# A convolution with a gated layer on one Trainium2 core: residual of two tile pairs moved to VectorE, gate weights loaded before four input tiles, idle products in halves, and a new order

## The chip, the cores and the metric

The kernel runs on one core of one Trainium2 chip. The core has five engines with instruction streams of their own: TensorE (PE, with its weight loads listed as PEld), VectorE (DVE), ScalarE (ACT), GpSimd (POOL) and SyncE (SP), which here only issues transfers. The metric is the device time of one execution in microseconds. A timing is the median of several executions; a profile is one execution more, recorded by the hardware profiler.

## The reference

The input `A_u` has 2048 rows of 512 channels. It is normalised by rows, and three things are added: the input itself, a long convolution over the rows (one kernel per channel, made of 128 complex modes), and a gated layer of inner width 1792.

```python
x  = A_u                                   # 2048 x 512
xn = _layernorm(x)
# convolution: kernel per channel from A, B, C and dt
logdA = exp(log_dt)[:, None] * (A_re + 1j * A_im)
P  = exp(logdA[:, :, None] * arange(L))
K  = einsum("dn,dnl,dn->dl", Cc, P, dt * Bc).real
y  = irfft(rfft(pad(xn)) * rfft(pad(K)))[:L] + xn * Dskip
# gated layer
h  = sigmoid(xn @ w_gate) * (xn @ w_up)    # 2048 x 1792
out = x + y + h @ w_down
```

All inputs are bfloat16, and so is the output.

## The kernel before

**Planner and order.** The kernel does not issue instructions as its functions run. Each step is recorded by `pl.add(engine, cost, fn, deps, prio, acq, rel)` as an operation with a number (966 of them), with the operations it depends on and the buffer slots that it takes and gives back. `run()` then walks a list of all numbers, `ORDER`, which is written out in the file; slots are handed out first in, first out along the list. The list is thus the program order of every engine and queue at once; semaphores are set from the dependences. The costs and due times that the operations carry are not used once the list is there. Pools that matter here: `gu`, four PSUM banks for the products of the gated layer; `s`, two PSUM pairs (1024 columns) for all else; `ot`, three output tiles.

**Which engine.** Three tuples move single steps between engines. `UEV` lists those of the 56 up products (4 row groups of 512 rows by 14 tiles of the inner width) that ACT copies from PSUM to SBUF (L1072) before DVE multiplies them with the gate (L1076); for the others DVE reads the PSUM bank in the multiplication. `ON_DVE` lists the operations among copies (L285 on DVE, L287 on ACT), casts (L660, L662) and row normalisations that run on DVE rather than on ACT. `FIN_ACT` lists those of six tile pairs of the output for which the other summand is brought in by PE.

**Stages.** All loads of the start (L430 to L470) go to SP's queue, one behind the other. While they run, `keep_warm` (L516) gives PE idle products of 128×512 into a bank that nobody reads. `layernorm` (L531) normalises the rows: tiles x0 to x3 (128 rows each) early, and transposes them by PE into `xnT`; x4 to x15 go out to a scratch in DRAM and come back transposed. The parameters (`par`, two loads) pass through a chain on DVE and ACT (L609 to L634, `f_w0` and `f_g` among it) to the first power of the modes, and a ladder of squarings (L664 to L679) makes eleven more; casts put them into the tables `W`. The convolution is a transform in two steps: first products over row tiles (`fx`, L685 on) are stored to `z_scr`; the convolution kernel's terms are built by DVE in four parts (c = 0 to 3, L747 to L843); then for each of two channel halves (p = 0, 1) and eight units a tile of `z_scr` is loaded and transformed (L882), swapped, multiplied with the kernel's transform (L904, L909, L913), transformed back (`fv`, L926), copied from PSUM (L287) and stored to `v_scr`. From `v_scr` the tiles are loaded again (`reload`, L963 to L974) for the last step (`s2_mm`, L985 and L988). Between all these, PE works on the gated layer: gate products (L1036), up products (L1060), down products (L1105), group by group of 512 rows.

**The end.** For the first three row groups the down products are copied to `glu_sb`, the input rows are added to them by a transfer that accumulates, and `final` (L990) joins them, pair by pair of tiles, with the last step of the convolution:

```python
res = glu_sb[:, 2 * t:2 * t + 2, :] if t < 4 else ...
on = t in FIN_ACT
def fi():
    for r in range(2):
        T.matmul(bank(sl, r), ident[:], res[:, r, :], start=True, ...)
...
if on:      # ACT copies the sum out of PSUM (L1007)
else:       # DVE adds res to the PSUM sum (L1011)
```

With a pair in `FIN_ACT`, two products with an identity matrix (L999) put `res` into PSUM first, the convolution's products add to it, and ACT copies the pair out. Otherwise DVE adds `res` while it reads the pair. The last row group's down products go into the same bank as their convolution sums, and DVE adds the input rows (L1125); its last tile is done in two halves of 256 columns. Output stores go out on SP's queue, the very last on ACT's.

Of the kernel before, what the change touches and what calls it, by code (L numbers as in the profile page):

```python
# [44 lines left out]
FIN_ACT = (1, 3, 5,)  # L45
# [133 lines left out]
def _consts():  # L179
# [19 lines left out]
UEV = (0, 6, 7, 9, 11, 12, 13, 14, 15, 16, 17, 18, 19, 21, 23, 24, 25, 26, 28, 29, 30, 31, 32, 33, 34, 35, 36, 37, 38, 39, 40, 41, 43, 44, 46, 47, 49, 52, 54, 55,)  # L199
ON_DVE = (88, 91, 106, 108, 123, 124, 125, 139, 140, 186, 196, 197, 200, 201, 203,)  # L200
ON_ACT = (2,)
ORDER = [
# [43 lines left out]

class _Op:
    __slots__ = ("alt", "tab", "eng", "cost", "fn", "prio", "acq", "rel", "dma", "left", "users", "ready", "start", "done", "seq", "mode")

class _Slot:  # L250
    __slots__ = ("pool", "idx")

    def __init__(self, pool, idx=None):
        self.pool = pool
        self.idx = idx
# [62 lines left out]
def kernel(  # L318
# [197 lines left out]
    def keep_warm(n, prio):  # L516
        wsl = _Slot("gu")
# [229 lines left out]
    for c in range(4):  # L747
# [11 lines left out]
        n = 1  # L759
# [435 lines left out]
```

## Time and profile before

| | us |
|---|---|
| median of three timed runs | 217.75 |
| the three runs | 217.75, 217.63, 219.24 |
| the profiled execution | 219.51 |
| its span, first to last instruction | 217.6 |

The difference of 1.9 us between the profiled execution and its span lies around the instructions. The granted PE clock is full (1.00) in the whole span. An engine's busy time is the union of its instructions; a wait is time in which the engine stood with its next instruction blocked, put down to what released it. In lists of instructions the form is: engine, line, operation, result tile, operand tiles, shape and count; in the timeline, start and length stand in front. "SPq" and "ACTq" are issues of transfers; a transfer's landing is told from its issue.

### The profile page before, as it was taken

The page shows a single profiled execution, that of the slowest core. Times are in us where ns is not written, and L with a number is a line of the kernel's source. Part 1 is how long each engine was busy: PE and PEld are TensorE (multiplying, and loading weights), DVE is VectorE, ACT ScalarE, POOL GpSimd, SP SyncE. Part 2 cuts the span into 40 slices and gives each one's busy share as a digit, 9 for nine tenths or more (in the row PEclk, how much of TensorE's full clock was granted, in tenths as well). Part 3 has the DMA queues.
Part 4 walks back from the last instruction along what each step waited for, and adds up shares of the span by engine and source line. Part 5 has one row for each costly group of instructions (what it writes and reads, how often), then busy time and mean ns, then how long its engine had stood idle before and what let it go on. Part 6 is the DMA issues. An engine that isn't in the chain of part 4 may idle for free.

```text
span 217.6 us, 4946 instructions
## 1 busy us (share of the span) xinstructions
PE 209.0 (96%) x1876; PEld 104.0 (48%) x1876; DVE 193.8 (89%) x438; ACT 179.5 (83%) x286; POOL 18.8 (9%) x40
## 2 busy tenths in 40 slices
PE   7979999999999999989999999999999999999894
PEld 2435444444444454435455565445546556544463
DVE  3989999999999999999999999999999999970433
ACT  3799999999999999869989999976897999960111
POOL 1410202002100020012000002010800000000000
PEclk9999999999999999999999999999999999999999
DMA  6999936001463689865697679929959969984974
GB/s 186 316 369 390 299 116 146 0 3 48 145 156 97 233 249 156 264 143 105 166 271 202 183 224 209 239 79 216 216 116 252 282 188 263 267 245 139 269 256 166
DMA packets 51530, 42.80 MB, mean 197 GB/s; under 512 B 16434, under 2 KB 43571, under 8 KB 51507
## 3 DMA queue, kind: packets, MB, share of 16 engines
q1 hardware_dynamic: 50338, 40.60, 63.8%
q0 software_dynamic: 864, 1.57, 5.5%
q10 hardware_dynamic: 304, 0.33, 0.6%
q8 instruction: 14, 0.23, 0.4%
q14 instruction: 10, 0.07, 0.1%
HBM read 25.97 MB, written 12.85 MB: 178 GB/s over the span
## 4 chain that ended last, share of the span: by engine, by line
PE 64%; DMA 17%; ACT 8%; SPq 7%; issue 2%; DVE 0%; ACTq 0%
PE bank L1060 18%; PE bank L1036 16%; PE bank L1105 10%; PE pair L904 7%; SPq L421 7%; DMA wu_sb<-in_B_w_up_dram 5%; PE pair L926 4%; ACT big L287 4%; DMA z_scr<-big 3%; DMA big<-big 3%; DMA big<-z_scr 2%; DMA v_scr<-big 2%; PE pair L882 2%; PE pair L820 2%; ACT us_sb L1072 2%
## 5 line engine op out<-in xcount | busy, mean ns | idle before, releaser
L287 ACT ACTIVATE big<-pair 128x1024 bf16<-128x1024 f32 x64 | 66.2, 1060 | 4.9 <-PE pair L926 1.5
L1060 PE MATMUL bank<-xnT,wu_sb 128*128 128x512 bf16 x224 | 54.5, 380 | 0.5 <-DMA wu_sb<-in_B_w_up_dram 0.4
L1036 PE MATMUL bank<-xnT,wg_sb 128*128 128x512 bf16 (+1 forms) x220 | 50.7, 368 | 1.9 <-DMA wg_sb<-in_B_w_gate_dram 1.8
L1105 PE MATMUL bank<-wd_sb,hT_sb 128*128 128x512 bf16 (+1 forms) x238 | 50.4, 367 | 0.0
L1036 PEld LDWEIGHTS <-wg_sb 128*128 128x128 bf16 x236 | 22.2, 98 | 26.9 <-issue 2.5
L1105 PEld LDWEIGHTS <-hT_sb 128*128 128x128 bf16 x238 | 22.6, 98 | 25.2 <-issue 1.9
L1060 PEld LDWEIGHTS <-wu_sb 128*128 128x128 bf16 x224 | 20.6, 98 | 25.2 <-issue 3.0
L1048 ACT ACTIVATE hT_sb<-bank 128x512 bf16<-128x512 f32 x52 | 30.9, 636 | 1.2 <-PE bank L1036 1.1
L735 DVE TENSOR_TENSOR big<-big 128x1024 bf16<-128x1024 bf16 (+4 forms) x40 | 26.8, 670 | 0.3 <-ACT big L287 0.2
L736 DVE TENSOR_TENSOR big<-big 128x1024 bf16<-128x1024 bf16 (+4 forms) x40 | 26.7, 667 | 0.0
L1072 ACT ACTIVATE us_sb<-bank 128x512 bf16<-128x512 f32 x40 | 25.9, 648 | 0.3
L909 DVE TENSOR_TENSOR big<-big 128x2048 bf16<-128x2048 bf16 x16 | 19.5, 1218 | 0.6 <-PE pair L926 0.3
L904 PE MATMUL pair<-big 128*128 128x256 bf16 x160 | 19.8, 273 | 0.0
L789 ACT ACTIVATE sq_sb<-big 128x256 bf16<-128x256 bf16 (+2 forms) x20 | 13.8, 691 | 5.1 <-DVE big L741 4.9
L904 PEld LDWEIGHTS <-big 128*128 128x128 bf16 x160 | 15.4, 98 | 4.9 <-issue 1.0
L1076 DVE TENSOR_TENSOR hT_sb<-hT_sb,us_sb 128x512 bf16<-128x512 bf16 x40 | 16.5, 418 | 0.4 <-ACT us_sb L1072 0.3
L740 DVE TENSOR_TENSOR big<-big 128x512 bf16<-128x512 bf16 (+4 forms) x40 | 16.5, 414 | 0.1
L741 DVE TENSOR_TENSOR big<-big 128x512 bf16<-128x512 bf16 (+4 forms) x40 | 16.5, 413 | 0.0
L1007 ACT ACTIVATE big<-pair 128x1024 bf16<-128x1024 f32 x3 | 3.1, 1023 | 15.2 <-PE pair L985 12.4
L895 DVE COPY big<-big 32x1024 bf16<-32x1024 bf16 x32 | 13.4, 419 | 0.6
L1011 DVE TENSOR_TENSOR big<-pair,glu_sb 128x1024 bf16<-128x1024 f32 x2 | 2.5, 1226 | 11.7 <-PE pair L985 8.1
L541 DVE BATCH_NORM_STATS2 stats<-big 128x6 f32<-128x512 bf16 x15 | 9.8, 682 | 3.4 <-DMA big<-in_A_u_dram 3.4
(104 smaller groups left out, 244.3 us busy)
## 6 DMA issues: line engine op xcount, KB each, us to landing
big<-c_E SPq DMA_DIRECT2D x16, 320.0 KB, 3.9
z_scr<-big SPq DMA_DIRECT2D x16, 256.0 KB, 2.9
big<-z_scr SPq DMA_DIRECT2D x16, 256.0 KB, 4.9
v_scr<-big SPq DMA_DIRECT2D x16, 256.0 KB, 3.1
big<-in_A_u_dram SPq DMA_DIRECT2D x4, 512.0 KB, 8.2
big<-big SPq DMA_DIRECT2D x32, 64.0 KB, 3.6
wu_sb<-in_B_w_up_dram SPq DMA_DIRECT2D x2, 896.0 KB, 10.7
wd_sb<-in_B_w_down_dram SPq DMA_DIRECT2D x1, 1792.0 KB, 15.1
```

The source lines that it names most:

```text
L287: nc.scalar.activation(out=get(out), in_=get(in_), func=ACT.Identity)
L735: V.tensor_tensor(out=wide(outp), in0=wide(lo), in1=mre, op=ALU.mult)
L736: V.tensor_tensor(out=wide(tb()), in0=wide(lo), in1=mim, op=ALU.mult)
L740: V.tensor_tensor(out=outp[:, :, 0], in0=outp[:, :, 0], in1=tb()[:, :, 1], op=opr)
L741: V.tensor_tensor(out=outp[:, :, 1], in0=outp[:, :, 1], in1=tb()[:, :, 0], op=opi)
L904: T.matmul(two(sk)[:, o:o + DW], es()[:, g, kt, :], kTv[p][:, :, kt, :], start=kt in (0, NKT - 1), stop=kt >= NKT - 2)
L909: V.tensor_tensor(out=pp().rearrange("p q h m -> p (q h) m"), in0=xx().rearrange("p q h m -> p (q h) m"), in1=kb()[:, 0:2 * DW].unsqueeze( ...
L1036: T.matmul(bank(sl, k % 2)[:, c0:c1], w[:, kt, k * 128:(k + 1) * 128], xnT[:, grp, kt, c0:c1], start=(kt == 0), stop=(kt == KT - 1))
L1048: S.activation(out=hT_sb[:, hs.idx, k % 2, :], in_=bank(sl), func=ACT.Sigmoid)
L1060: T.matmul(bank(sl), wu_sb[:, kt, k * 128:(k + 1) * 128], xnT[:, grp, kt, :], start=(kt == 0), stop=(kt == KT - 1))
L1072: S.activation(out=us_sb[:, us.idx, :], in_=bank(sl), func=ACT.Identity)
L1105: T.matmul(bank(po)[:, 0:c[1] - c[0]], hT_sb[:, hts[k // 2].idx, k % 2, jj * 128:(jj + 1) * 128], wd_sb[:, k, c[0]:c[1]], start=first and ...
```

## The change

Six things differ:

1. `FIN_ACT` goes from (1, 3, 5) to (5,): tile pairs 1 and 3 lose their identity products (two operations, four matmuls), and DVE adds `res` for them in place of ACT's copy.
2. `UEV` has 38 members rather than 40, and others.
3. `ON_DVE` is another set: the ladder's cast of k = 10, one copy of `gc` and a seed copy go to ACT; three seed copies come to DVE; of the row normalisations, tiles 4 and 6 are on DVE in place of 5 and 7, and tile 8 in place of 12.
4. `keep_warm` does its products in halves of 256 columns where it has more than one.
5. The order of the loads on SP's queue. Before: x0, x1, x2–3, `dskr`, `par` (A), identity, x4–7 (512 KB), first gate piece (896 KB, the largest), `par` (B and C), the two other gate pieces, up weights first half, second half, x8–11, x12–15, down weights. After: x1, x0, x2–3, `par` (A), identity, first gate piece, x4–7, `par` (B and C), the other gate pieces, up weights second half, x8–11, the table S1, x12–15, up weights first half, down weights; `dskr` comes later.
6. The rest of the list is reordered on every engine. On PE the idle product at 27.81 us moves to the start, with six instead of four between the transposes. On SP, near the end, the stores of the last three units to `v_scr` stand directly behind one another, ahead of the loads that bring `v_scr` back for the second channel half; before, a load of 384 KB stood ahead of the last store.

```diff
-FIN_ACT = (1, 3, 5,)
+FIN_ACT = (5,)
...
-UEV = (0, 6, 7, 9, 11, 12, 13, 14, 15, 16, 17, 18, 19, 21, 23, 24, 25, 26, 28, 29, 30, 31, 32, 33, 34, 35, 36, 37, 38, 39, 40, 41, 43, 44, 46, 47, 49, 52, 54, 55,)
-ON_DVE = (88, 91, 106, 108, 123, 124, 125, 139, 140, 186, 196, 197, 200, 201, 203,)
+UEV = (1, 7, 9, 10, 11, 12, 13, 15, 16, 17, 18, 19, 20, 22, 24, 25, 28, 29, 30, 31, 32, 33, 34, 35, 36, 37, 38, 39, 40, 41, 42, 46, 48, 49, 50, 52, 53, 55,)
+ON_DVE = (88, 105, 107, 122, 123, 124, 125, 140, 197, 198, 199, 200, 201, 202, 203,)
 ORDER = [
-    0, 1, 2, 14, 28, 38, 26, 29, 27, 3, 30, 39, 49, 32, 31, 40, 33, 41, 35, 18, 34, 4, 42, 43, 50, 24, 10, 44, 19,
...
-    956, 864, 962, 872, 869, 868, 963, 870, 957, 871, 960, 873, 874, 875, 961, 964, 965]
+    1, 28, 18, 0, 24, 2, 3, 26, 29, 38, 27, 30, 31, 32, 39, 33, 4, 49, 40, 34, 41, 43, 35, 22, 42, 50, 36, 44, 51,
...
+    863, 954, 870, 867, 868, 866, 871, 955, 869, 960, 961, 959, 872, 962, 873, 963]
...
         def fn():
-            for _ in range(n):
-                T.matmul(bank(wsl), glu_sb[:, 0, 0:128], glu_sb[:, 0, :], start=True, stop=True)
+            w = 256 if n > 1 else 512
+            for c in range(0, 512 * n, w):
+                cs = slice(c % 512, c % 512 + w)
+                T.matmul(bank(wsl)[:, cs], glu_sb[:, 0, 0:128], glu_sb[:, 0, cs], start=True, stop=True)
```

The operations behind the second dropped one keep their place in the kernel's text and have numbers lower by one or two, so the two lists cannot be compared number by number at their end. Lines behind L519 have numbers higher by two in the changed kernel.

82 rows, old and new, of the table ORDER are left out of this document.

## The prediction

> **What bounds the kernel now.** I read the page first, then the waits of TensorE (PE), then the three stages as windows, then the chain in order of time at both ends.
>
> ```profile
> span 217.6 us, 4946 instructions
> PE 209.0 (96%) x1876; PEld 104.0 (48%) x1876; DVE 193.8 (89%) x438; ACT 179.5 (83%) x286; POOL 18.8 (9%) x40
> ...
> GB/s 186 316 369 390 299 116 146 0 3 48 145 156 97 233 249 156 264 143 105 166 271 202 183 224 209 239 79 216 216 116 252 282 188 263 267 245 139 269 256 166
> ...
> PE 64%; DMA 17%; ACT 8%; SPq 7%; issue 2%; DVE 0%; ACTq 0%
> ```
>
> PE is busy for 96% and carries most of the chain; what is left of the chain is mostly transfers. Where PE waits:
>
> ```profile
> PE bank L1036 <- DMA wg_sb<-in_B_w_gate_dram: 1.8, 1, 1.8
> ...
> PE pair L985 <- DMA big<-v_scr: 0.8, 1, 0.8
> ```
>
> ```profile
> 10.00:190.00 180.00, 176.82 (x1653) 87.34 (x1654) 176.91 (x401) 167.66 (x271) 16.24 (x29) 1.00 0.70 191
> ...
> 200.00:214.50 14.50, 13.61 (x121) 8.46 (x119) 5.80 (x7) 3.07 (x3) 0.00 (x0) 1.00 0.77 231
> ```
>
> The columns are the stretch, its length, then busy time of PE, weight load, DVE, ACT and POOL, and the granted clock. From 10 to 190 us DVE is as full as PE: each is idle about 3.1 us of 180 (180 − 176.9), ACT 12.3. From 200 us on, only PE is full (13.61 of 14.5); DVE has 8.7 and ACT 11.4 idle. So work taken from PE shortens the tail at once, while in the middle PE and DVE have to gain together.
>
> **The start: gate weights ahead of input rows.**
>
> ```profile
> 2.11 0.34 SPq L421 DMA_DIRECT2D dskr<-in_A_Dskip_dram  x1
> ...
> 3.84 0.43 SPq L421 DMA_DIRECT2D wg_sb<-in_B_w_gate_dram  x1
> ...
> 4.87 2.69 SPq L421 DMA_DIRECT2D wg_sb<-in_B_w_gate_dram  x2
> ```
>
> ```profile
> DMA to landing us min/median/max: 8.6/10.4/10.9
> ```
>
> ```profile
> 1.43 6.87 PE L521 MATMUL bank<-glu_sb 128*128 128x512 bf16 x18 [1.43 <-POOL rz L515]
> ...
> 12.50 3.63 PE L1036 MATMUL bank<-xnT,wg_sb 128*128 128x512 bf16 x16 [1.80 <-DMA wg_sb<-in_B_w_gate_dram]
> ...
> 18.13 2.77 PE L1036 MATMUL bank<-xnT,wg_sb 128*128 128x256 bf16 x20
> 21.32 1.04 PE L1060 MATMUL bank<-xnT,wu_sb 128*128 128x512 bf16 x4 [0.42 <-DMA wu_sb<-in_B_w_up_dram]
> ...
> 27.81 0.38 PE L521 MATMUL bank<-glu_sb 128*128 128x512 bf16 x1
> 28.03 1.89 PE L1060 MATMUL bank<-xnT,wu_sb 128*128 128x512 bf16 x8
> ```
>
> The first gate weights are issued at 3.84 and land 8.6 later, at 12.45; PE starts on them at 12.50 after waiting 1.80. The change puts x4–7 (512 KB) behind them. At the 369 to 390 GB/s of those slices 512 KB take 1.4 us, so they land at about 11.1; the removed issue of dskr (0.34) goes too, but the data, not the issues, are late here. The transposed rows allow it:
>
> ```profile
> 10.35 0.68 DVE L573 COPY xnT<-pair 128x1024 bf16<-128x1024 bf16 x1
> 10.95 1.87 DVE L541 BATCH_NORM_STATS2 stats<-big 128x6 f32<-128x512 bf16 x3
> ...
> 13.79 1.29 DVE L609 TENSOR_TENSOR big<-big 128x512 f32<-128x512 bf16 x2 [0.90 <-DMA big<-in_A_par_dram]
> ...
> 15.61 0.68 DVE L634 TENSOR_TENSOR big<-big 128x512 f32<-128x512 f32 x1
> ...
> 18.14 0.69 DVE L541 BATCH_NORM_STATS2 stats<-big 128x6 f32<-128x512 bf16 x1
> ```
>
> xnT is complete at 11.03 (10.35 + 0.68). So the first gate starts near 11.2, 1.3 earlier. Not all is kept: the other two gate pieces have as many bytes ahead of them as before and land at about 15.3 and 16.5 (4.87 + 10.4; the second issue + 10.9), so four gates of 0.86 (3.63 for four) are through at 14.7 and PE waits some 0.6 and then 0.3. The up weights come in two halves of 896 KB, 2.4 us each at that rate. Before, the half that PE asks for first came second, and PE waited for it at 21.32 (0.42). Now it comes first and lands about 16.5 + 2.4 = 18.9, ahead of the first up product, which the gates hold until about 19.4: no wait. The other half goes behind x8–15 (1 MB): 18.9 + 2 × 1.4 + 2.4 ≈ 24.1, and the new order asks for it some two microseconds later; if that is too late, PE waits there instead. Moreover the idle product at 27.81 leaves the busy stretch: 0.22, by the start of the next row (28.03 − 27.81). Sum at 30 us: 1.3 − 0.9 + 0.42 + 0.22 ≈ 1.0 of lead. Bounds: 0 if the queue serves the pieces side by side, 2.4 if both waits (1.80 + 0.42) and the product go.
>
> What it costs: x4–7 now land where the weights landed, near 12.45. DVE took three of their statistics from 10.95 while it waited for the parameters anyway (0.90 until 13.79). With all four (0.6 each) behind 12.45, the parameter products (f_g, L609) start near 14.9 instead of 13.79, and the ladder's start, over at 16.29 (15.61 + 0.68), ends near 17.4: 1.1 later, of which 0.6 is the fourth statistic (at 18.14 before) done ahead and so given back. The rest, 0.5, is lost time of a full engine. PE's next need of the ladder is the kernel generation, with gate and up products between as cover.
>
> Halving the idle products keeps their columns, and all of them now sit in the first 11 us, where PE waits for rows; so do the two more idle products between the transposes and x1 loaded ahead of x0 (three equal loads in one row of issues). Priced at zero; the cover is that wait for the first gate weights. If it were gone, the two products would cost 0.22 each. That they no longer warm the array I count in no case: the granted clock is 1.00 in the windows, with gaps of 1.80 us before.
>
> **The middle.** Work changes hands both ways.
>
> ```profile
> L1072 ACT ACTIVATE us_sb<-bank 128x512 bf16<-128x512 f32 x40 | 25.9, 648 | 0.3
> L1076 DVE TENSOR_TENSOR hT_sb<-hT_sb,us_sb 128x512 bf16<-128x512 bf16 x40 | 16.5, 418 | 0.4 <-ACT us_sb L1072 0.3
> ...
> L1076 DVE TENSOR_TENSOR hT_sb<-hT_sb,bank 128x512 bf16<-128x512 bf16 x16 | 10.8, 679 | 0.4 <-PE bank L1060 0.4
> ```
>
> Two up products more are read by DVE from PSUM: 2 × (679 − 418) = +0.52 us on DVE, 2 × 648 = −1.3 on ACT. Against it a ladder cast goes from DVE to ACT and small seeds, copies and row normalisations swap sides; I cost their sum at −0.5 on DVE (one 128x512 cast, about a statistic's 0.6, away; three seeds of under 0.2 to it), so DVE's total stands still, within ±0.6. DVE has only 3.1 us idle between 10 and 190, so PE can keep of its lead only what DVE finds in that idle: less than half. I take 0.4 of the 1.0, from −0.8 (the late rows' 0.5 plus order losses) to +1.0. Otherwise the new order puts nearly the same work of each engine ahead of the same milestones (the kernel products, the last transforms, the last store), stores and reloads of z and k among it, so I cost the rest of it at nothing; its cover is the 3.1 us of idle, and without that a slip in one engine's list is paid in full, which the −0.8 allows for.
>
> **The tail.**
>
> ```profile
> 192.39 0.80 PE pair L926 x16
> ...
> 193.26 1.03 ACT big L287
> ...
> 194.31 4.82 DMA v_scr<-big
> ...
> 199.21 3.05 DMA big<-v_scr
> ...
> 202.30 0.52 PE pair L985 x6
> ...
> 204.35 3.13 PE bank L1105 x14
> 207.48 0.43 PE pair L999 x2
> ```
>
> ```profile
> 192.21 0.60 SPq L421 DMA_DIRECT2D big<-v_scr  x1
> ...
> 195.03 6.22 PE L1105 MATMUL bank<-wd_sb,hT_sb 128*128 128x512 bf16 x28
> ```
>
> ```profile
> v_scr<-big SPq DMA_DIRECT2D x16, 256.0 KB, 3.1
> ```
>
> ```profile
> L1007 ACT ACTIVATE big<-pair 128x1024 bf16<-128x1024 f32 x3 | 3.1, 1023 | 15.2 <-PE pair L985 12.4
> L1011 DVE TENSOR_TENSOR big<-pair,glu_sb 128x1024 bf16<-128x1024 f32 x2 | 2.5, 1226 | 11.7 <-PE pair L985 8.1
> ```
>
> The last product of the second transform ends at 193.19, its eviction at 194.29, its store lands 4.82 later and the reload 3.05 after that: 9.1 us. The store's median is 3.1; it took 4.82 with a reload of 384 KB issued just ahead of it (192.21) on the same queue. In the new order the last stores stand back to back ahead of that reload: 3.1 to 3.3, so 9.1 becomes about 7.6, with 0.15 for two evictions in a row 7.75. The reloads moved behind the stores are asked for by the sums from 202.30 on, and with 3.05 for one have room. The cover that PE then has is 28 down products (6.22), one up product (four matmuls, 0.86 as the gates) and small ones, some 7.4; the first identity pair (0.43) is no longer in it. So the data stay late by a little, and the gain is 9.1 − 7.75 ≈ 1.35. From 0 (the store stays at 4.82; 0.43 less work only makes PE wait longer) to 1.4.
>
> The second identity pair (207.48) lies on the path after the data are in: 0.43, with its switching 0.5. In exchange DVE adds the residual of two pairs: 1.23 each instead of ACT's 1.02. In that stretch DVE has 8.7 us idle and waits 8.1 for these very sums, so 2.5 fits beside PE; if that cover were gone, 0.2 a pair, or 1.2 if they queued ahead of the last output adds. VectorE: DVE Perf Modes, Specifications, in the Trainium skill, speaks against both moves: ScalarE sits closer to PSUM, VectorE closer to SBUF. The rows agree in size (1226 against 1023 ns, 679 against 418); by the rule alone the edit would be a loss of 0.4, which holds only were DVE the bound there.
>
> **Sum.** −0.4 − 1.35 − 0.5 = −2.25. The profiled execution took 219.51: its span of 217.6 and 1.9 around it; so 217.3 for it. It stands 0.8% above the median of the three runs, 217.75, and I carry the difference over, not the level: 215.5, and 0.3 for stalls of the new order that the rows of the old one cannot show makes 215.8.
>
> **Rivals.**
> 1. Only PE's removed work counts. The start's lead dies in the full DVE, and the store still needs 4.8. For: DVE is at 176.91 of 180; other stores are in flight beside it. Against: the 3.1 median. Then −0.5: 217.2.
> 2. Slower: the input rows behind the weights hold DVE's in-order queue. If x4–7 land at 13.3 instead of 12.45 or the whole 1.1 is lost, the loss runs through a DVE without slack to the last product, and the tail saves only its 0.5: 217.75 + 1.1 to 2.6 − 0.5 = 218.4 to 219.9, middle 218.8. It decides from a ladder start later than about 17.4. For: DVE is full. Against: 0.6 of the delay is work done ahead.
> 3. Everything gained: 2.4 at the start with DVE following, 1.4, 0.5: 217.75 − 3.6, with 0.7 lost on the way 214.2. Against: DVE loses no work.
>
> **Numbers.** Forecast 0.45, rival 1 0.21, rival 2 0.17, rival 3 0.17. The range 213.9 to 218.8 leaves out the far half of rival 2 and of rival 3. One per cent, 2.2 us, is about what a measurement here tells from no change: faster means under 215.6. That holds for rival 3 and for less than half of the forecast (0.17 + 0.2 = 0.37); slower, over 219.9, for the end of rival 2 and an unseen stall: 0.10; within 0.53.
>
> **What would show it.** First gate near 11.2; ladder start over near 17.4; the last store under 3.5 us; no PE wait before the first reloaded product; DVE waiting, not PE, at the residual adds. The forecast is wrong if DVE's last product comes later than PE's lead allows, or a new wait stands in PE's list between 30 and 190.

## The result, and the profile after

| | before | after |
|---|---|---|
| median, us | 218.13 (four runs, 217.63 to 219.24) | 220.63 (four runs, 220.02 to 221.16) |
| ratio after to before | | 1.0102, 95% interval 1.006 to 1.0144 |
| profiled execution, and its span | 219.51, 217.6 | 220.60, 218.4 |

The change makes the kernel 1.0% slower; 0.9% faster was predicted. Throughout, a ratio is taken to the kernel before on the same chip and leaves disturbed runs out, so it need not be the quotient of two medians.

The profile before that the prediction was made from was 1.4 us above the median of its kernel. The unchanged kernel was therefore run and profiled again (218.30, span 216.2); that second profile is the better measure, and is called "before, second profile". First the page of the kernel after: span, busy time, the queue that brings instructions (packets, MB, share of 16 engines), and the shares of the chain that ended last.

```profile
span 218.4 us, 4989 instructions
...
PE 209.0 (96%) x1895; PEld 106.7 (49%) x1895; DVE 196.7 (90%) x439; ACT 177.5 (81%) x283; POOL 23.4 (11%) x40
...
q8 instruction: 15, 0.25, 0.6%
...
DVE 45%; PE 23%; ACT 17%; DMA 9%; issue 3%; SPq 1%; DVEq 0%; ACTq 0%
```

The chain went for 64% over PE before (65% in the second profile); now it goes for 45% over DVE. PE has 19 products more (23 by the halves, less the four of the two identity pairs), and q8 brings one piece of instructions more, 15 for 14. The waits of PE in the kernel after (in total, times, longest), without the one at the very start (1.4, as before):

```profile
PE bank L1038 <- ACT us_sb L1074: 0.5, 2, 0.3
PE bank L1038 <- DVE xnT L575: 0.5, 1, 0.5
PE bank L1062 <- DVE hT_sb L1078: 0.4, 1, 0.4
PE pair L906 <- issue: 0.4, 1, 0.4
PE pair L884 <- DMA big<-z_scr: 0.3, 1, 0.3
...
PE pair L1038 <- DMA wg_sb<-in_B_w_gate_dram: 0.2, 1, 0.2
```

The waits of 1.80 for the gate weights and 0.8 for the reloaded tiles are gone. Others stand in the middle: for a tile of `z_scr` at 97.66, for ACT's copies of up products at 105.17 and 108.98, one put down to "issue" (no semaphore) at 133.85, and one for DVE at 158.45. The start as the timeline shows it (start, length), first PE and then DVE:

```profile
11.26 3.61 PE L1038 MATMUL bank<-xnT,wg_sb 128*128 128x512 bf16 x16 [0.48 <-DVE xnT L575]
...
19.29 1.03 PE L1062 MATMUL bank<-xnT,wu_sb 128*128 128x512 bf16 x4
```

```profile
12.20 1.88 DVE L543 BATCH_NORM_STATS2 stats<-big 128x6 f32<-128x512 bf16 x3 [1.09 <-DMA big<-in_A_u_dram]
...
16.65 0.69 DVE L636 TENSOR_TENSOR big<-big 128x512 f32<-128x512 f32 x1
```

PE begins the gates at 11.26 instead of 12.50, and the up products at 19.29. DVE stands 1.09 for the input rows, and the ladder's start is over at 17.33 (16.65 + 0.69) instead of 16.29. The stretches of the middle and of the end:

```profile
10.00:190.00 180.00, 177.25 (x1644) 87.26 (x1642) 176.64 (x394) 166.25 (x267) 20.98 (x29) 1.00 0.69 192
...
200.00:214.50 14.50, 13.21 (x121) 8.51 (x119) 8.55 (x10) 0.09 (x1) 0.00 (x0) 1.00 0.79 230
```

DVE is as full as before in the middle (176.64 of 180), and has taken over what ACT did at the end (8.55, against ACT's 0.09). Now the chain of the kernel after, in order of time, from the first sum of reloaded tiles on:

```profile
201.62 0.61 PE pair L987 x8
...
203.45 1.23 DVE big L1013
...
204.70 3.38 DMA out_dram<-big
...
208.71 1.22 DVE big L1013
...
209.95 4.30 DMA out_dram<-big
...
214.41 1.02 ACT big L1009
```

It runs through an output store of 4.30 us, and ends in an eviction by ACT that waited for that store. In ACT's timeline, after and in the second profile before:

```profile
214.41 1.02 ACT L1009 ACTIVATE big<-pair 128x1024 bf16<-128x1024 f32 x1 [18.26 <-DMA out_dram<-big]
```

```profile
211.59 1.02 ACT L1007 ACTIVATE big<-pair 128x1024 bf16<-128x1024 f32 x1 [2.69 <-PE pair L985]
```

It is the last tile pair, 5, whose sum ACT copies out of PSUM. There are three output tiles (`ot`); pair 5 gets the one that the store of pair 3 frees. In the second profile before, that store leaves at 208.93 and takes 2.30; it has landed 0.36 before the eviction, and ACT waits for PE only. The margin is thin: in the first profile the store already ended ACT's wait, and the eviction began 0.19 behind the end of its sums (213.03 for 212.84) instead of 0.09. After, the sum is there and the tile is not. DVE's last output add hardly moves between the same two:

```profile
213.24 0.42 DVE L1127 TENSOR_TENSOR big<-bank,big 128x256 bf16<-128x256 f32 x1 [0.41 <-PE bank L1107]
```

```profile
213.18 0.42 DVE L1125 TENSOR_TENSOR big<-bank,big 128x256 bf16<-128x256 f32 x1 [0.95 <-PE bank L1105]
```

So the milestones lie like this (us; ends, where nothing else is said):

| | before, second | after | difference | summed up in the prediction |
|---|---|---|---|---|
| first gate starts | 12.48 | 11.26 | −1.22 | −1.3 |
| ladder's start | 16.26 | 17.33 | +1.07 | +1.1 |
| last transform back (`fv`) | 192.90 | 193.97 | +1.07 | −0.4 |
| last store to `v_scr` landed | 197.23 | 198.02 | +0.79 | −1.75 |
| pair 0 added | 203.04 | 203.54 | +0.50 | |
| pair 3 added or copied | 208.90 | 209.92 | +1.02 | |
| pair 5's eviction starts | 211.59 | 214.41 | +2.82 | |
| last output add of DVE | 213.60 | 213.67 | +0.07 | |
| last store landed | 215.24 | 217.47 | +2.23 | −2.25 |

Both steps of the start came as predicted, and by 194 us the lead had turned into a delay. The computation itself recovered from it (two identity pairs of 0.43 are out of PE's list), and the 2.23 us stand at the very end, in one eviction and its store.

### The profile page after: what moved, and what is told of

It reads as the page before. It is cut to its first block, busy times and chain, and to the rows that moved or that the text cites. A ratio compares the mean times of both kernels' runs of the same rounds, so it can differ in the third digit from the quotient of the medians.

```text
span 218.4 us, 4989 instructions
## 1 busy us (share of the span) xinstructions
PE 209.0 (96%) x1895; PEld 106.7 (49%) x1895; DVE 196.7 (90%) x439; ACT 177.5 (81%) x283; POOL 23.4 (11%) x40
## 4 chain that ended last, share of the span: by engine, by line
DVE 45%; PE 23%; ACT 17%; DMA 9%; issue 3%; SPq 1%; DVEq 0%; ACTq 0%
DVE big L737 8%; DVE big L738 8%; PE bank L1062 5%; PE bank L1038 5%; PE pair L906 5%; DVE hT_sb L1078 5%; DVE big L743 4%; DVE big L742 4%; DMA big<-in_A_u_dram 4%; DMA out_dram<-big 4%; PE pair L928 3%; ACT big L664 3%; PE bank L1107 3%; ACT big L287 3%; ACT big L670 2%
## 5 line engine op out<-in xcount | busy, mean ns | idle before, releaser
L287 ACT ACTIVATE big<-pair 128x1024 bf16<-128x1024 f32 x64 | 64.6, 1035 | 5.8 <-PE pair L906 1.9
L1074 ACT ACTIVATE us_sb<-bank 128x512 bf16<-128x512 f32 x38 | 23.0, 616 | 1.5 <-DVE hT_sb L1078 1.0
L1009 ACT ACTIVATE big<-pair 128x1024 bf16<-128x1024 f32 x1 | 1.0, 1024 | 18.3 <-DMA out_dram<-big 18.3
L1078 DVE TENSOR_TENSOR hT_sb<-hT_sb,us_sb 128x512 bf16<-128x512 bf16 x38 | 15.5, 417 | 0.0
L664 ACT ACTIVATE big<-big 128x512 bf16<-128x512 f32 x22 | 12.8, 649 | 0.0
## 6 DMA issues: line engine op xcount, KB each, us to landing
wd_sb<-in_B_w_down_dram SPq DMA_DIRECT2D x1, 1792.0 KB, 15.3
```

The lines of the kernel that those rows point to most:

```text
L287: nc.scalar.activation(out=get(out), in_=get(in_), func=ACT.Identity)
L1074: S.activation(out=us_sb[:, us.idx, :], in_=bank(sl), func=ACT.Identity)
L1078: V.tensor_tensor(out=h(), in0=h(), in1=us_sb[:, us.idx, :] if on else bank(sl), op=ALU.mult)
```

## The experiments

### The kernel before, once more: before_again

Nothing is edited.

> The kernel before, unchanged, profiled a second time. Theory: its first profile (219.51 us) caught the last store to v_scr at 4.82 us, 1.4 above the timed runs; a second profile shows that store at about 3 us, a span near 216 us and 14 code fetches on queue q8. Rival: the 4.82 us belongs to the kernel and comes again, with a span near 217.6.

Ratio 1.0 (0.9967 to 1.0034). Its issues by SP:

```profile
194.05 0.37 SPq L421 DMA_DIRECT2D v_scr<-big  x1
...
194.80 4.34 SPq L421 DMA_DIRECT2D big<-v_scr  x4
```

The last store is issued at 194.05 and lands at 197.23: 3.18, with the same load of 384 KB ahead of it that the prediction blamed. The 4.82 was a matter of that one execution: in the eight further profiles of kernels with before's list, or nearly, the last store takes 2.81 to 3.78. In the transfer records of the first profile a piece of instructions of 16 KB (q8) moved for 1.6 us from 196.04, inside that store; in the second one it started at 196.36 and took 0.89.

### The idle products: after_whole, before_halves, after_quarters

after_whole puts whole products back into the changed kernel, as shown here; before_halves puts the halves alone into the kernel before, the same edit the other way round:

```diff
-            w = 256 if n > 1 else 512
-            for c in range(0, 512 * n, w):
-                cs = slice(c % 512, c % 512 + w)
-                T.matmul(bank(wsl)[:, cs], glu_sb[:, 0, 0:128], glu_sb[:, 0, cs], start=True, stop=True)
+            for _ in range(n):
+                T.matmul(bank(wsl), glu_sb[:, 0, 0:128], glu_sb[:, 0, :], start=True, stop=True)
```

> The changed kernel with the idle products whole again (23 products and 23 weight loads less on PE, same columns). Theory: the 15th code fetch of PE (q8, 16 KB, 1.76 us at 210.96) is gone, the store of output pair 3 lands in about 2.3 us instead of 4.3, the last ACT eviction starts 1.5 to 2 us earlier, and the time falls by 1.5 to 2 us, to about 218.7. Rival (the fetch is harmless, the output slot or the moved residual is the cause): the time stays within 0.5 us of 220.6 and the store at 4 us.

Ratio 1.0244 (1.0195 to 1.0293): slower by another 1.4%, though it does 23 products less. PE's timeline and one of the windows of after_whole:

```profile
154.55 1.68 PE L820 MATMUL pair<-big 128*32 128x82 bf16 x121
160.34 0.33 PE L820 MATMUL pair<-big 128*32 128x82 bf16 x7 [4.11 <-issue]
160.60 1.89 PE L1036 MATMUL bank<-xnT,wg_sb 128*128 128x512 bf16 x4
```

```profile
160.30:166.50 6.20, 6.16 (x27) 1.76 (x27) 2.27 (x4) 2.92 (x4) 0.00 (x0) 0.51 0.54 122
```

PE stands still for 4.11 us inside a burst of 128 very small products (part of the convolution kernel's terms), "issue", that is, no semaphore holds it. From 160.3 to 166.5 the granted clock is 0.51. Four gate products take 1.89 rather than 1.03. The transfer records of this profile have the pieces of instructions around it:

```
q8 136.08 took 998 ns, 16384 bytes
q8 157.86 took 893 ns, 16384 bytes
q8 161.38 took 1020 ns, 16384 bytes
```

In the kernel after, where there is no such stall, the one in the middle came at 150.97, and in the second profile before at 152.55. So the reading is that the instructions ran out: 121 of the 128 products pass within 1.68 us, and the next piece is fetched too late. That the form of the idle products decides it is shown; that the late fetch is the cause is read from the records, and not all of it: the piece was through at 158.75, and PE went on only at 160.34.

> The kernel before with the idle products in halves and nothing else. Theory (code fetch): PE passes 1876 + 23 products, so a 15th fetch appears on q8 some 20 to 25 products before the end (around 212 us) and meets the last output stores: 0.7 to 2 us slower. Rival: the halves cost nothing, within 0.5 us of before.

Ratio 1.0144 (1.0069 to 1.0218). The halves do cost in the kernel before too; with runs from 219.10 to 221.99. Its profile is of the fastest one (219.10, against 218.30 in the second profile before), so it shows only 0.8 us of the 3 that 1.4% are. It has 15 pieces of instructions for 14, and the same wait for the tile as the kernel after, shorter; the eviction starts 0.74 later than in the second profile before (212.33 for 211.59):

```profile
212.33 1.02 ACT L1009 ACTIVATE big<-pair 128x1024 bf16<-128x1024 f32 x1 [2.90 <-DMA out_dram<-big]
```

after_quarters makes the same columns in products of 128, 46 products more than after, so that the pieces begin elsewhere:

```diff
-            w = 256 if n > 1 else 512
+            w = 128 if n > 1 else 512
```

> The changed kernel with the idle products in quarters of 128 columns instead of halves: 46 products and 46 weight loads more at the start, same columns, nothing else. It moves PE's 15th code fetch some 46 products earlier in the work, to about 206.5 us, away from the store of output pair 3. Theory (the fetch on that store's transfer engine makes the last eviction wait): the store lands in about 2.3 us, the eviction of pair 5 starts near 212.3 instead of 214.4, the time falls by 1 to 1.6 us to about 219.2. Rival (the wait comes from the order or from three output tiles alone): within 0.5 us of 220.6.

Ratio 1.0075 (1.0033 to 1.0116): 0.3% below that of after, less than the 1 to 1.6 us expected, and the two intervals overlap. In the trace the last piece comes at 208.99 and is through before the store of pair 3 leaves at 210.96. ACT's timeline:

```profile
213.13 1.02 ACT L1009 ACTIVATE big<-pair 128x1024 bf16<-128x1024 f32 x1 [16.00 <-DMA out_dram<-big]
```

From that store's start to the eviction are 2.17 us, where the kernel after has 4.46 (214.41 − 209.95). The eviction still waits for the tile, but briefly.

### The transfer that held the store

The kernel after, from the issue of pair 3's store to its landing: busy share of the 16 transfer engines in 40 slices, and the queues.

```profile
DMA  9995100379978920000018993101010001999999
...
q1 hardware_dynamic: 495, 0.78, 49.7%
q8 instruction: 1, 0.02, 2.6%
```

The output stores share this stretch with one piece of instructions. From the middle on, most slices are nearly empty: few engines have anything left, and the stores are not yet done. The records of the long packets there:

```
q8 210.96 took 1759 ns, 16384 bytes
q1 212.70 took  232 ns,  2048 bytes
q1 212.92 took  227 ns,  2048 bytes
q1 213.13 took  212 ns,  2048 bytes
```

Three last packets start one behind the other when the piece of instructions is through, as on one engine; the records do not name the engine. In before_halves it is the other way round: the piece starts at 211.69, just when a row of six such packets ends (each 0.154, the last from 211.53), and the store there takes 2.77. Over the kernels, a store of pair 3 that has a piece beside it takes 4.30 (after, piece at 210.96), 4.10 (after_rows_first, 211.92) and 4.35 (after_nofin, 211.94); without one 2.31 (before_fin), and about 2 in after_quarters.

### The residual and the output tiles: after_ot4, before_ot4, before_fin, before_fin_ot4, after_nofin

after_ot4 gives the changed kernel a fourth output tile, so that no eviction waits for a store; before_ot4 does the same to the kernel before.

```diff
-... vs=2, ot=3, tg=2 ...
+... vs=2, ot=4, tg=2 ...
```

> The changed kernel with four output tiles instead of three, so that the last eviction need not wait for the store of output pair 3. Theory: whatever slows that store, the eviction of pair 5 starts right behind its sums (near 211.6 instead of 214.4) and the end is then set by the last DVE add and its store: 1.2 to 2 us faster than the changed kernel, about 218.8. Rival (the end waits for the stores themselves): within 0.5 us of 220.6.

Ratio 1.0058 (1.0019 to 1.0096). The eviction now waits for its sum and starts 2.2 earlier, with a piece of instructions still there, at 212.46:

```profile
212.22 1.02 ACT L1009 ACTIVATE big<-pair 128x1024 bf16<-128x1024 f32 x1 [15.92 <-PE pair L987]
```

So the wait for the tile is worth 0.44% (1.0102 − 1.0058), some 1.0 us, though the two intervals overlap; 0.6% is left. The chain shows by which way it reaches the end here:

```profile
192.69 0.80 PE pair L928 x16
...
194.44 1.03 ACT big L287
...
195.48 2.83 DMA v_scr<-big
...
198.38 3.88 DMA big<-v_scr
...
202.30 0.95 PE pair L987 x14
```

It is the path of the prediction: the last transform back, its eviction, the store, the reload, and PE waiting (0.30) for the tiles. In the second profile before, PE begins these sums at 200.92 and waits for none of it.

> The kernel before with four output tiles instead of three. Control for the fourth tile: in the kernel before, the eviction of pair 5 waits for a slot too, but the last DVE add and its store end later. Theory: no change, within 0.3 us of before. Rival (a fourth tile helps any order): 0.7 us or more faster.

Ratio 0.9977 (0.9935 to 1.0018): in the kernel before a fourth tile gains nothing that can be measured. DVE does wait 1.61 for a store in the second profile before (ahead of an add at 210.07), but the chain of that profile runs over PE up to the last add.

before_fin makes the move of the residual alone, in the order of before:

```diff
-FIN_ACT = (1, 3, 5,)
+FIN_ACT = (5,)
...
-858, 865 in ORDER (the identity products)
```

> The kernel before with only the tuple of residual pairs changed to (5,): pairs 1 and 3 lose their identity products and are added by DVE at the places in the order where ACT copied them. Theory (PE alone is full in the tail): 0.4 to 0.9 us faster than before. Rival (DVE becomes late in the tail, or the last eviction waits for a slot as in the changed kernel): same or up to 1.5 us slower.

Ratio 1.0049 (1.001 to 1.0089): two identity pairs of 0.43 us are gone, and there is no gain. DVE's timeline, the chain and ACT's timeline:

```profile
207.07 2.36 DVE L968 TENSOR_TENSOR big<-pair,glu_sb 128x1024 bf16<-128x1024 f32 x2 [2.04 <-PE pair L942]
```

```profile
209.46 0.33 SPq L378
...
209.84 2.31 DMA out_dram<-big
```

```profile
212.32 1.02 ACT L964 ACTIVATE big<-pair 128x1024 bf16<-128x1024 f32 x1 [17.42 <-DMA out_dram<-big]
```

(The lines are lower by 43 here, as the list is written in one line.) DVE now adds pairs 2 and 3 one after the other, 2.36, where pair 3 was ACT's before; on SP's queue pair 3's store stands behind pair 2's until 209.84, 0.9 later than in the second profile before (208.93). The eviction of pair 5 has to wait for it, without any piece of instructions in the way.

> The kernel before with the residual tuple (5,) and four output tiles. Theory (moving the residual made the kernel before 0.5% slower only because the last eviction then waited for the store of pair 3): the loss goes, and the identity products' time comes out: 0.2 to 0.6 us faster than before. Rival (DVE's adds themselves are late): still 0.5 to 1 us slower than before.

Ratio 0.9982 (0.9946 to 1.0018), beside 1.0049 with three tiles, the two intervals just meeting: the two adds in a row cost something only through the tile.

after_nofin takes this one move back out of the changed kernel: `FIN_ACT` is (1, 3, 5) again, with the identity products right ahead of their sums.

> The changed kernel with only the residual tuple put back to (1, 3, 5): the identity products of pairs 1 and 3 stand again right ahead of their sums and ACT copies both pairs. Theory (the add of pair 3 behind that of pair 2 on DVE sends its store off 0.9 us later, into PE's 15th code fetch, and the last eviction waits for that store): the store leaves near 209, lands before 212, the eviction of pair 5 starts before 212.5; the two identity pairs cost 0.5 to 1; in all 0.5 to 1.4 us faster than the changed kernel, about 219.6. Rival, as I predicted (identity products on the path, DVE's adds free): 0.5 to 0.9 us slower than the changed kernel, about 221.3.

Ratio 1.0138 (1.0092 to 1.0184), not faster than after. The sum of pair 3 is late here too, and its store meets the piece of instructions. The chain:

```profile
210.56 4.35 DMA out_dram<-big
...
215.02 1.02 ACT big L966
```

A gain would have needed ACT's copy of pair 3 to come earlier than DVE's add. With the identity products on PE's path it does not: its store leaves 0.6 later than in after (210.56 for 209.95). By the trace the identity products do cost PE time, as predicted; the ratios of the two kernels overlap.

### The order of the loads: before_weights_first, after_rows_first

In both, the numbers 10 (x4–7) and 11 (first gate piece) change places in `ORDER`, and nothing else.

> The kernel before with two loads swapped: the first gate weights ahead of the four input tiles. Theory (DVE sets the pace up to the last transform, so an earlier first gate is worth nothing there, while DVE stands idle longer): first gate about 1.3 us earlier, ladder start about 1 us later, the time unchanged to 0.5 us slower. Rival, as I predicted: 0.4 to 1 us faster.

Ratio 0.9974 (0.9922 to 1.0026). The first gate starts at 11.06. The ladder's start ended at 15.3 here, earlier than before rather than later, because both loads landed sooner in this execution than in others (x4–7 at 10.94). It shows no loss by the swap, and no gain that could be measured; the delay of the ladder could not be tested in it.

> The changed kernel with those two loads put back: the four input tiles ahead of the first gate weights. Theory (DVE sets the pace): first gate 1.2 us later, ladder start about 1 us earlier, the last transform 0.2 to 0.5 us earlier, the time equal or up to 0.5 us faster. Rival (PE sets the pace): 0.5 to 1.2 us slower.

Ratio 1.0123 (1.0058 to 1.0188). The ladder's start is over at 15.76, 1.6 earlier than in after, and DVE ends the last unit's product at 192.91, against 193.08. The end is held by the store as in after. By time the two cannot be told apart; in the trace 0.17 of the 1.6 is left at 193 us.

### How full DVE is: before_dve_more, after_ot4_dve_less, before_fin_ot4_dve_less

before_dve_more takes 8 up products (16, 19, 23, 28, 32, 39, 43, 47) out of `UEV` in the kernel before, so that DVE reads them from PSUM.

> The kernel before with eight more up products (16, 19, 23, 28, 32, 39, 43, 47) read from PSUM by DVE instead of being copied by ACT first: DVE has 8 x 0.26 = 2.1 us more, ACT 8 x 0.65 = 5.2 us less. Theory (DVE sets the pace up to the last transform, without slack): 1.2 to 2.2 us slower than before. Rival (PE sets it, and DVE's lists have room): within 0.5 us of before.

Ratio 1.0153 (1.008 to 1.0226). Up to 198 us DVE is busy 2.36 us longer than in the second profile before (189.76 for 187.40), and its list ahead of the tail ends 2.82 later (197.42 for 194.60): work added to DVE goes into the time in full. (The edit also frees ACT and makes the PSUM bank wait for DVE; that is not told apart.) In the kernel after the same list ends at 195.66, 1.06 later than in the second profile before; it begins 0.36 earlier, and has 0.74 us more work (188.14) and 0.69 more idle time.

The reverse was then tried, more up products copied by ACT: 23, 27 and 45 with after_ot4, and 48, 50 and 51 with before_fin_ot4.

> The changed kernel with four output tiles and three more up products (23, 27, 45) copied by ACT: DVE has 0.78 us less to do. Theory (the rest of the loss is DVE's): 0.4 to 0.8 us faster than the changed kernel with four tiles, 0.3% over before. Rival (PE or ACT sets it): no change, 0.6% over before, or slower by ACT's added 1.9 us.

Ratio 1.0161 (1.0107 to 1.0216), a miss. DVE's waits in it:

```profile
DVE hT_sb L1078 <- ACT us_sb L1074: 1.9, 2, 1.0
```

Against after_ot4 DVE has 0.55 us less work and 1.86 more idle time. In the written order ACT's copies come too late for the multiplications that now need them.

> The kernel before with the residual tuple (5,), four output tiles and three more up products (48, 50, 51) copied by ACT. Theory (DVE sets the pace): 0.4 to 0.8 us faster than the same kernel without them, 0.3 to 0.6% faster than before. Rival: no faster than it, 0.2% faster than before.

Ratio 1.0063 (1.0028 to 1.0098), a miss in the same way: against before_fin_ot4, 0.78 less work and 3.27 more idle time; DVE waits 3.5 for ACT, where it waited 0.2. So neither run tells what DVE's time alone is worth: in both lists the copies moved to ACT come too late.

### Two together: after_quarters_ot4, before_wf_fin_ot4

after_quarters_ot4 has the products of 128 columns and the fourth tile.

> The changed kernel with quarters and four output tiles. Theory (the moved code fetch and the fourth tile take away the same wait): as the changed kernel with four tiles alone, 0.4 to 0.8% over before. Rival (two causes that add up): 0.2% over before or less.

Ratio 1.0055 (1.0019 to 1.0091), that of after_ot4 alone: both take away the same wait. About 0.55% remains that neither touches.

before_wf_fin_ot4 puts into the kernel before what had looked harmless: the weights first, the residual on DVE, a fourth tile.

> The kernel before with the residual tuple (5,), four output tiles, and the first gate weights ahead of the four input tiles. Theory: the two gains add up, 0.5 to 1.2 us faster than before and the fastest of all so far, about 217.2. Rival (DVE sets the pace and the input rows come late): as the same kernel without the swapped loads, or slower.

Ratio 0.998 (0.9951 to 1.0008), that of the kernel without the swapped loads (0.9982), so the gains did not add up. No version here beats the kernel before by more than the measurement can tell.

## Why the prediction was wrong

**The start: right.** The gates were to begin near 11.2 and began at 11.26; the ladder's start was to end near 17.4 and ended at 17.33; the first up product came at 19.29 without a wait, as forecast. The two waits for the later gate pieces, put at 0.6 and 0.3, were 0.19 and 0.15. DVE was busy 0.23 us less by 30 us than in the second profile before (25.01 for 25.24), where the prediction had 0.5 of "lost time of a full engine"; by 80 us it had made that up (74.77 for 74.75).

**The middle: this step failed first.** "PE can keep of its lead only what DVE finds in that idle", and 0.4 was taken as kept; "DVE's total stands still, within ±0.6"; and the rest of the new order was cost "at nothing". The last transform back ended 1.07 later than in the second profile before, and DVE's list 1.06 later. The loss lies between 80 and 160 us, where the kernel's terms are built: there PE is busy for 78.31 us, against 79.56 in the second profile before and 79.13 in the first, and DVE for 78.93, against 79.66 and 79.54. PE waits there 0.26 for a tile of `z_scr` (the first profile before has 0.7 for one), 0.53 for two of ACT's copies, 0.41 put down to "issue", and 0.41 for DVE. The last three kinds come again in after_ot4 and after_nofin, at nearly the same places, where PE is busy for 78.71 and 78.08; the second profile before has a single wait of 0.25 in this stretch. In the second profile before and in after (stretch, length, busy time of PE, granted clock):

```profile
80.00:160.00 80.00, 79.56 (x882) 1.00 0.76 191
```

```profile
80.00:160.00 80.00, 78.31 (x871) 1.00 0.76 196
```

So the term put at nothing is the one that failed, and a new wait in PE's list between 30 and 190 us is what the prediction itself named as a sign that it is wrong.

DVE also got 0.74 us more work ahead of the tail, just above the bound, and before_dve_more shows that such work costs its full time. That the waits and this work make up the 0.6% left in after_ot4 fits in size, but isn't shown: no run took the waits out or gave DVE its time back, since both attempts made it wait for ACT. How much belongs to DVE's work and how much to the order is open.

**The store: a term that wasn't there.** The 1.35 came from one store of 4.82, in an execution 0.8% above the median. "I carry the difference over" took a mishap of that profile as a property of the kernel: the second profile has 3.18. Two evictions in a row were put at 0.15; ACT's eviction of the last unit begins at 193.00 in the second profile before and, as the second of a pair of 1.94 from 193.37, at 194.29 in after. The queue of two evictions costs 0.22 beyond the late transform, and the store takes 2.69, under the 3.5 that was named; so the new order loses 0.79 up to the last landing instead of gaining. The wait before the first reloaded product is gone, as forecast, but the second profile before has none there either:

```profile
200.92 0.30 PE L985 MATMUL pair<-xnT,big 128*64 128x256 bf16 x2
```

This wait comes and goes in both orders: it is 1.1 in before_ot4 and 1.0 in before_wf_fin_ot4, and 0.3 in after_ot4 and 1.0 in after_rows_first. One profile of each kernel cannot price it.

**The identity products: right for PE, wrong for the end.** "2.5 fits beside PE" holds for DVE's time. But the sentence behind it named the price, "1.2 if they queued", and what queued was not the output adds but pair 3 behind pair 2, then its store on SP, then pair 5 for the tile. The prediction never asked who gets the tile that pair 3 gives back. Its own lines held a hint: of the 15.2 idle ahead of ACT's copies only 12.4 ended with the sums, and of DVE's 11.7 only 8.1; the rest, 2.8 and 3.6, ended with an output store. That wait, with the store stretched by a piece of instructions, is, by the two ratios, the 0.44% of after_ot4. Of the 0.5 taken for an identity pair 0.43 is the row; no row shows the 0.07 of "switching". In before's order with four tiles the move costs nothing that can be measured.

**The halves: priced at zero for the wrong reason.** Their time was indeed hidden: PE still waited 0.48 ahead of the first gate, now for the transposed rows. But 23 more products and as many weight loads shift every later instruction of PE against the pieces in which instructions are fetched. With whole products the changed kernel stalls for 4.1 us, and with halves a 15th piece falls on the store at the end.

**The rivals.** The slower rival came nearest in sign. Its place, input rows that hold DVE's queue, is not confirmed: the ladder's start was over at 17.33, not later than the 17.4 that it asks for, and with the rows first the ladder is 1.6 earlier and the last unit 0.17 sooner. (The middle of its 218.4 to 219.9 is 219.1, not 218.8.) The first rival, by which the start's lead dies, was right in that; its price left the tile and the new waits out.

## What to carry to other kernels

Profile the unchanged kernel twice before a single long transfer becomes a term of a sum. When a step moves to another engine, follow its result as far as its buffer: who waits for the tile that its store frees, and how far ahead of that it lands. Adding instructions to an engine's stream, idle ones too, moves where its code is fetched, so compare variants of a count before reading a change of one per cent as the effect of anything else.

## What the runs showed of the hardware

A piece of PE's instructions is one packet of 16,384 bytes, on a queue (q8) that the profile counts on the same 16 transfer engines as the data; before_halves, which adds nothing but products and weight loads to PE, has 15 of them for 14. A piece took 0.88 to 2.2 us. A store of data that has one beside it took 4.10 to 4.35 us in three kernels of the new order (2.77 in before_halves, where the piece comes late), for 2.31 without, and the packet times fit a store whose last packets stand behind the piece. The Trainium skill, Runtime: NRT & Kernel Launch, Instruction fetch mechanics, has the block of 16 KiB, which agrees, and calls the cost of crossing into the next one mostly hidden; here it was not hidden at the store, nor, by the reading above, in after_whole, where PE stood for 4.11 us.

In that stall PE stood from 156.23 on. The granted clock was 1.00 up to 159.56 and 0.50 from there to 166.39, for 6.83 us, of which PE worked for 6.04, while the wait of 1.80 us at 10.7 in the kernel before left it at 1.00. The Trainium skill, TensorE: Matmul & The Clock Gate, Part 1, has the clock halved after an idle window of about 3.4 us and restored after at least one busy window of as much, the windows running free of the kernel. Both waits agree, the clock falling 3.33 us into the long one and not at all in the short one; the slow stretch is as long as two windows, which that rule leaves room for.
